# Random-feature attention and a GELU network in one kernel: the instruction order made anew, and sums of weights formed in the x buffer

## The chip, the core and the metric

The kernel runs on one core of a Trainium2 chip. The metric is the time of one execution on the device, in microseconds (us). The engines are PE (TensorE, matrix products), DVE (VectorE), ACT (ScalarE), POOL (GpSimd) and SP (SyncE, which here only issues DMA transfers).

## What is computed

Eight batches of eight heads with 576 tokens of 64 numbers go through attention with exponential features, and the result through a network of two matrix products. Everything is in float32. The core of the reference:

```python
def phi(x):
    proj = np.einsum('bhsd,df->bhsf', x, w_phi)                      # 128 features
    proj = proj - np.max(np.abs(proj), axis=-1, keepdims=True)
    return np.concatenate([np.exp(proj), np.exp(-proj)], axis=-1)
q_p, k_p = phi(q), phi(k)
kv = np.einsum('bhsf,bhsd->bhfd', k_p, v);  z = np.sum(k_p, axis=2)
num = np.einsum('bhsf,bhfd->bhsd', q_p, kv)
den = np.einsum('bhsf,bhf->bhs', q_p, z)[..., None] + 1e-06
x = (num / den) laid out as 4608 tokens of 512
h = x @ w_in;  g = 0.5 * h * (1.0 + erf(h * inv_sqrt2));  out = g @ w_out   # 512 -> 2048 -> 512
```

## The kernel before, in words

**The network** works on 18 blocks of 256 tokens. A number is split into a high part that PE's fast float32 form takes whole and a low rest, so a product is three matrix products (high by high, low by high, high by low). Block j waits for its x: the loads into `xr`, one buffer for all blocks, and of the quotients' denominators into `xh`; then three DVE rows: `xr` times `xh` (L375), a cast to `xh` (L371), and the difference to `xl` (L375). Then, for eight pairs of columns u: `ph_j_u` (24 products of 256 columns), two GELUs on ACT, the difference `gl_j_u` on DVE (it reads `ph`, which is in PSUM), and the second products `po` with `gh`, `gl` and `w_o`. Blocks 8 to 17 (`seven`) form the second product with seven products in place of eight; for that they need five sums or differences of quarters of each pair of `w_o`, 40 in all, which `sums_of_weights` makes earlier, stores in HBM, and `fetch_sums` loads back.

**The weights** `w_in` and `w_out` come as 64-bit numbers in 32 tiles. `split_weight` makes each into two float32r halves: ACT takes the magnitude (L390), DVE does two rows of the form TENSOR_SCALAR (L391, L393) and two of SCALAR_TENSOR_TENSOR (L395, L397) on `wt`, ACT copies the high half (L369), and DVE takes the difference (`w_i..` or `w_o.. <- wt,w`, L375), the last row of a tile.

**The attention** of batch b runs among the blocks: `pk`, `mx`, `ek`, `kv` for the keys, and `pq`, `pc`, `mb`, `ef`, `pn`, `xo` for the queries. `mb` (L511, a maximum over partitions) and, from batch 2 on, `db` (L522, a sum over partitions that gives the denominators) are partition all-reduces on GpSimd. `db` reads `pc` after two TENSOR_SCALAR rows (L553) and two SCALAR_TENSOR_TENSOR rows (L556) of DVE have formed it. A name such as `pc_2_1_0` means batch 2, pair of heads 1, piece 0.

**The order.** The kernel writes down several thousand operations with their reads and writes; `Plan.order` then gives all engines their order by a list schedule with modelled costs and priorities (`rank`), and `emit` issues them so. Each engine runs its own queue strictly in that order on the chip; waits are by semaphores. Of GpSimd and DVE the schedule has a model: `port` is the time at which DVE's last row that works on SBUF alone ends, and `READS` and `SPENT` are how long an all-reduce reads and lasts. A DVE row with `port` that would fall into an all-reduce's reading is put behind it:

```python
if o.eng == "pool" and o.port:
    t = max(t, port[0])
...
if o.eng == "dve" and o.port and port[1] <= t < port[2]:
    t = port[2]
```

Rows of DVE that read PSUM (`mx`, `ek`, `gl`) are made with `port=False`.

Of the kernel before, what the change touches and what calls it, by code (L numbers as in the profile page):

```python
# [62 lines left out]
class Plan:  # L63
# [49 lines left out]
    def order(self, bias):  # L113
# [178 lines left out]
def fused_kernel(ctx: ExitStack, tc: tile.TileContext, qT, kT, va, w_st, w_in, w_out, out):  # L292
# [436 lines left out]
    def sums_of_weights(rank):  # L729
# [3 lines left out]
        for k in range(NFC // 2):  # L733
            d = Buf(plan, None, lambda k=k: dpool.tile([P, 5, 2, HDM], F32, name=f"t_d{k}"))
            stored.append(d)
            a, b = wo[k], wo[k + 8]
            for i, (x, xc, y, yc, o) in enumerate((
                    (b, low_cols, a, high_cols, ALU.add), (b, low_cols, b, high_cols, ALU.add), (a, low_cols, a, high_cols, ALU.add),
                    (b, high_cols, a, high_cols, ALU.subtract), (a, low_cols, b, low_cols, ALU.subtract))):
# [4 lines left out]
                plain, low, high = (lambda t=t: t().bitcast(F32)), (lambda t=t: t()[:, 0, :]), (lambda t=t: t()[:, 1, :])  # L744
# [3 lines left out]
                tt("dve", dve(HDM), low, lambda low=low: low().bitcast(F32), lambda high=high: high().bitcast(F32), ALU.subtract, [t], [t], **kw)  # L748
                op("sp", 0.06, lambda d=d, i=i, plain=plain: nc.sync.dma_start(out=d()[:, i], in_=plain()), r=[t], w=[d], kb=262, **kw)
# [185 lines left out]
```

## Time and profile before

| | us |
|---|---|
| median of 3 runs (lowest, highest) | 1087.42 (1086.15, 1088.69) |
| the profiled execution | 1086.7 |
| its span, first to last instruction | 1084.9 |
| PE busy, share of the span | 1038.2, 96% |
| DVE busy | 697.5, 64% |
| ACT busy | 616.5, 57% |
| POOL busy | 305.4, 28% |

The span is what the trace covers, from the first to the last instruction; the execution's own time is 1.8 us longer. PE is busy nearly all of the time, so the kernel's time is PE's work, plus PE's waits, plus what PE loses while the chip grants it half of its clock.

### The profile page before, as it was taken

Reading aid. Unit: us, or ns where it says so; the run is one execution under the profiler, and the core shown is the slowest. Engines: PE = TensorE matmul, PEld = TensorE weight load, DVE = VectorE, ACT = ScalarE, POOL = GpSimd, SP = SyncE. Lnnn points to the kernel's source line nnn. Section 1 sums busy time; section 2 is a strip of 40 time slices with the busy share of each in tenths; the row PEclk is TensorE's granted clock in tenths of the full one; section 3 lists DMA queues with packets and bytes.
Section 4 is the critical chain, followed back from the end, with each engine's and each line's share of the span. In section 5 each row is a group of like instructions: output and inputs, shape, how many; then the busy total and the mean of one; then the engine's idle time right before and its main releaser. Section 6 shows DMA issues by size and latency. Waiting matters only on the chain.

```text
span 1084.9 us, 23613 instructions
## 1 busy us (share of the span) xinstructions
PE 1038.2 (96%) x9763; PEld 900.0 (83%) x9763; DVE 697.5 (64%) x1228; ACT 616.5 (57%) x1008; POOL 305.4 (28%) x77
## 2 busy tenths in 40 slices
PE   7979995999998999999999999999999999999997
PEld 5646664787786787777788879999999999999997
DVE  5999999688977788665344332555565565565554
ACT  4868785666666687667656653434344344344343
POOL 2232234346556453564654451000000000000000
PEclk7999998999999999999999999999999999999999
DMA  8486660344444335324212145620120120120000
GB/s 285 137 249 190 175 218 27 96 134 134 131 128 130 112 127 146 103 66 124 58 55 75 35 126 173 214 59 20 40 60 11 50 60 16 45 59 20 21 21 21
DMA packets 87180, 107.08 MB, mean 99 GB/s; under 512 B 29168, under 2 KB 56832, under 8 KB 87072
## 3 DMA queue, kind: packets, MB, share of 16 engines
q1 hardware_dynamic: 86928, 105.30, 31.9%
q8 instruction: 77, 1.26, 0.5%
q14 instruction: 31, 0.25, 0.1%
q10 hardware_dynamic: 144, 0.26, 0.1%
HBM read 75.87 MB, written 29.66 MB: 97 GB/s over the span
## 4 chain that ended last, share of the span: by engine, by line
PE 80%; DVE 8%; DMA 4%; ACT 3%; issue 3%; POOL 1%; SPq 0%; DVEq 0%; ACTq 0%; POOLq 0%
PE ph L334 33%; PE po L334 14%; PE pa L334 10%; PE pb L334 7%; PE kv L334 5%; PE pn L334 4%; PE pk L334 2%; PE pq L334 2%; DMA xh<-r_d 1%; DMA x_d<-xo 1%; DVE pc L375 1%; DVE pc L553 1%; DVE ts L375 1%; PE pn_rest L334 1%; POOL mb L511 1%
## 5 line engine op out<-in xcount | busy, mean ns | idle before, releaser
L334 PE MATMUL ph<-xh,w_i 128*128 128x256 f32 x2304 | 419.8, 279 | 7.0 <-DVE w_i L375 5.1
L334 PEld LDWEIGHTS ph<-xh,w_i 128*128 128x128 f32 x2304 | 359.4, 189 | 21.0 <-issue 12.2
L334 PE MATMUL ph<-xl,w_i 128*128 128x256 f32 x1152 | 320.1, 278 | 0.0
L334 PEld LDWEIGHTS ph<-xl,w_i 128*128 128x128 f32 x1152 | 217.9, 189 | 0.3
L522 POOL PARTITION_ALL_REDUCE db<-pc x24 | 151.0, 6290 | 137.2 <-DVE pc L556 112.7
L375 DVE TENSOR_TENSOR sg<-ga 128x256 f32<-128x256 f32 (+1 forms) x240 | 84.6, 376 | 153.2 <-ACT ga L780 151.4
L334 PE MATMUL po<-w_o,gh 128*128 128x512 f32 (+1 forms) x518 | 165.8, 402 | 5.0 <-DVE w_o L375 5.0
L511 POOL PARTITION_ALL_REDUCE mb<-pc x36 | 121.2, 3368 | 161.9 <-ACT pc L369 128.2
L780 ACT ACTIVATE ga<-ph 128x512 f32<-128x512 f32 x80 | 47.8, 598 | 168.7 <-PE ph L334 168.7
L334 PEld LDWEIGHTS po<-w_o,gh 128*128 128x128 f32 x518 | 94.5, 190 | 34.4 <-DVE w_o L375 5.3
L334 PE MATMUL pa<-w_o,oh 128*128 128x256 f32 x640 | 112.8, 276 | 0.0
L334 PE MATMUL po<-w_o,gl 128*128 128x512 f32 (+1 forms) x281 | 102.9, 381 | 7.1 <-DVE gl L375 7.1
L334 PEld LDWEIGHTS pa<-w_o,oh 128*128 128x128 f32 x640 | 96.3, 188 | 0.0
L334 PE MATMUL pa<-w_o,ol 128*128 128x256 f32 x320 | 88.3, 276 | 0.0
L375 DVE TENSOR_TENSOR gl<-ph,gh 128x512 fp32r<-128x512 f32 x64 | 43.7, 685 | 67.5 <-ACT ph L704 67.5
L334 PE MATMUL pn<-ef,kvn 128*64 128x512 f32 (+2 forms) x288 | 80.5, 561 | 5.6 <-ACT xo L369 5.6
L334 PE MATMUL pb<-tw,uh 128*128 128x256 f32 x480 | 85.6, 276 | 0.0
L516 ACT ACTIVATE ef<-pc 128x1024 f32<-128x1024 f32 (+1 forms) x72 | 68.1, 972 | 17.5 <-DVE pc L375 17.2
L444 ACT ACTIVATE ek<-ek 128x1024 f32<-128x1024 f32 x64 | 67.6, 1058 | 15.5 <-DVE ek L375 15.0
L334 PEld LDWEIGHTS pb<-tw,uh 128*128 128x128 f32 x480 | 72.2, 188 | 0.0
L334 PEld LDWEIGHTS po<-w_o,gl 128*128 128x128 f32 x281 | 53.9, 192 | 21.3 <-DVE gl L375 9.6
L703 ACT ACTIVATE gh<-ph 128x512 fp32r<-128x512 f32 x64 | 38.2, 597 | 54.2 <-PE ph L334 52.1
(84 smaller groups left out, 1620.8 us busy)
## 6 DMA issues: line engine op xcount, KB each, us to landing
vt<-in_va_dram SPq DMA_DIRECT2D x32, 325.0 KB
t_d<-ts SPq DMA_DIRECT2D x40, 256.0 KB
out_dram<-ob SPq DMA_DIRECT2D x35, 256.0 KB
kt<-in_kT_dram SPq DMA_DIRECT2D x32, 256.0 KB
raw_i<-in_w_in_dram SPq DMA_DIRECT2D x16, 512.0 KB
raw_o<-in_w_out_dram SPq DMA_DIRECT2D x16, 512.0 KB
qt<-in_qT_dram SPq DMA_DIRECT2D x28, 256.0 KB
x_d<-xo SPq DMA_DIRECT2D x24, 256.0 KB
```

Source lines behind the costliest of these rows:

```text
L334: return tc.keep_in_program_order(nc.tensor.matmul(*a, **kw))
L375: op(eng, cost, lambda: e.tensor_tensor(out=dst(), in0=a(), in1=b(), op=o), r=r, w=w, **kw)
L444: op("act", act(256 * n), lambda s=s: nc.scalar.activation(e[s](), e[1](), AF.Exp, scale=1.0 - 2.0 * s), r=[e[1]], w=[e[s]], table="exp", ...
L511: op("pool", plan.SPENT[most], lambda: nc.gpsimd.partition_all_reduce(mb(), pc(), P, bass_isa.ReduceOp.absmax), r=[pc], w=[mb], port=most, ...
L516: op("act", act(2 * n), lambda s=s: nc.scalar.activation(ef[s](), pc(), AF.Exp, scale=1.0 - 2.0 * s), r=[pc], w=[ef[s]], table="exp", **k())
L522: op("pool", plan.SPENT[total], lambda: nc.gpsimd.partition_all_reduce(db(), pc()[:, :2], P, bass_isa.ReduceOp.add), r=[pc], w=[db], port= ...
L553: op("dve", dve(n, fast=True) + 0.06, lambda pc=pc, ef=ef, one=one, j=j: nc.vector.tensor_scalar(out=pc()[:, j], in0=ef[0]()[:, j], scalar ...
L703: op("act", act(2 * TB, True) + 0.016, lambda gh=gh, ph=ph: nc.scalar.activation(gh(), ph(), AF.Gelu), r=[ph], w=[gh], table="gelu", rank= ...
L780: op("act", act(2 * TB, True) + 0.037, lambda ph=ph, ga=ga: nc.scalar.activation(ga(), ph(), AF.Gelu), r=[ph_all], w=[ga], table="gelu", a ...
```

## The change

Four things change. GpSimd operations no longer wait in the schedule for DVE's port to be free before they start; they start when they are ready, and it is their reading that the schedule moves behind DVE's last row. Their costs are new, and at a tie GpSimd goes first. The sums of weights are formed from whole values: for each pair k two rows `wr_k` add the halves of `w_o k` and `w_o k+8` (512 numbers per partition each) into a buffer of the tag `xr`, the one in which x is scaled; then each of the five sums is one row of 256 from `wr`, the ACT copy, and one difference of 256 (before: one row of 512 straight from the halves and two of 256). Since blocks and sums now share `xr`, the loads of x for block 7 and later wait for the last sum (`behind=last_sum`). And the table of constants is new, so the whole order is. The core of the diff:

```diff
@@ order
-            if o.eng == "pool" and o.port:
-                t = max(t, port[0])
...
-                if best is None or key[1] < best[1]:
+                if best is None or key[1] < best[1] or key[1] == best[1] and e == "pool":
...
-            o.start, o.end = t, run(t, cost, o.duty) if o.eng == "pe" else t + cost
+            o.start = t
+            if o.eng == "pool" and o.port:
+                t = max(t, port[0])
+                port[1:] = [t, t + self.READS[o.port]]
+            o.end = run(t, cost, o.duty) if o.eng == "pe" else t + cost
...
-            clock[o.eng] = o.end + (0.45 if o.eng == "pool" else 0.0)
+            clock[o.eng] = o.end
@@ tokens
-            kw = dict(w=[xr], rank=rank(0) - 8)
+            kw = dict(w=[xr], rank=rank(0) - 8, behind=last_sum if j >= SEVEN - 1 else ())
@@ sums_of_weights, for each k
+            raw = sb["xr"]([P, 4, HDM], F32, f"wr_{k}")
+            plan.since = SUMSAT + SUMSEACH * n
+            for i, w in enumerate((wo[k], wo[k + 8])):
+                tt("dve", dve(2 * HDM), lambda raw=raw, i=i: raw()[:, 2 * i : 2 * i + 2].rearrange("p a t -> p (a t)"),
+                   lambda w=w: w().bitcast(F32)[:, 0], lambda w=w: w().bitcast(F32)[:, 1], ALU.add, [w], [raw], rank=rank(n / 40))
...
-                tt("dve", dve(2 * HDM), plain, lambda x=x, xc=xc: x().bitcast(F32)[:, :, xc], lambda y=y, yc=yc: y().bitcast(F32)[:, :, yc], o, [x, y], [t], **kw)
-                tt("dve", dve(HDM), lambda low=low: low().bitcast(F32), lambda low=low: low().bitcast(F32), lambda high=high: high().bitcast(F32), ALU.add, [t], [t], **kw)
-                copy("act", act(HDM), high, lambda low=low: low().bitcast(F32), [t], [t], **kw)
+                last_sum[:] = [tt("dve", dve(HDM), low, lambda raw=raw, x=x: raw()[:, x], lambda raw=raw, y=y: raw()[:, y], o, [raw], [t], **kw)]
+                copy("act", act(HDM), high, low, [t], [t], **kw)
@@ constants (8 change, two shown)
-SUMSAT = 177.8
+SUMSAT = 224.11
-T0 = 91.27
+T0 = 146.2
```

What the new order is, at three places of DVE's queue. The number at a name's end only counts tiles.

The first place is in block 0, where the last tile of `w_in` (`w_i3_3`) is finished; `ph_0_6` cannot run without it. Before, from the row that completes `pc_2_0_0`, which GpSimd's `db_2_0_0` then reads:

```order
L556 SCALAR_TENSOR_TENSOR pc_2_0_0_1686<-ef_2_0_0_1_1834,kvn_2_0_0_1376,pc_2_0_0_1686 128x512
L395 SCALAR_TENSOR_TENSOR wt_i3_3_1928<-raw_i3_3_1709,wt_i3_3_1928 128x512
L391 TENSOR_SCALAR wt_o12_1946<-wt_o12_1946 128x512
L397 SCALAR_TENSOR_TENSOR wt_i3_3_1928<-raw_i3_3_1709,wt_i3_3_1928 128x512
L393 TENSOR_SCALAR wt_o12_1946<-wt_o12_1946 128x512
L553 TENSOR_SCALAR pc_2_1_0_1729<-ef_2_1_0_0_1843,kvn_2_0_1_1649 128x512
L395 SCALAR_TENSOR_TENSOR wt_o12_1946<-raw_o12_1774,wt_o12_1946 128x512
L375 TENSOR_TENSOR w_i3_3_1959<-wt_i3_3_1928,w_i3_3_1959 128x512
L397 SCALAR_TENSOR_TENSOR wt_o12_1946<-raw_o12_1774,wt_o12_1946 128x512
```

The same place now:

```order
L556 SCALAR_TENSOR_TENSOR pc_2_0_0_1720<-ef_2_0_0_1_1855,kvn_2_0_0_1582,pc_2_0_0_1720 128x512
L375 TENSOR_TENSOR w_i3_3_1937<-wt_i3_3_1838,w_i3_3_1937 128x512
L439 TENSOR_REDUCE mx_2_1_1_1948<-pk_2_1_1_1872 128x8
L375 TENSOR_TENSOR ek_2_1_1_1_1965<-pk_2_1_1_1872,mx_2_1_1_1948 128x1024
L393 TENSOR_SCALAR wt_o12_1885<-wt_o12_1885 128x512
L391 TENSOR_SCALAR wt_o13_1950<-wt_o13_1950 128x512
L395 SCALAR_TENSOR_TENSOR wt_o12_1885<-raw_o12_1715,wt_o12_1885 128x512
L393 TENSOR_SCALAR wt_o13_1950<-wt_o13_1950 128x512
```

`w_i3_3` has moved from the seventh row behind `pc_2_0_0` to the first, and two rows that read PSUM follow it.

The second place is where the last tile of `w_out` (`w_o15`) is finished. Before, `pc_2_1_0`, which `db_2_1_0` reads, had been complete 18 rows ahead of this piece's last row (`db_2_1_0` itself waited for the transfer out of the one `db` buffer):

```order
L397 SCALAR_TENSOR_TENSOR wt_o14_1986<-raw_o14_1870,wt_o14_1986 128x512
L391 TENSOR_SCALAR wt_o15_2084<-wt_o15_2084 128x512
L393 TENSOR_SCALAR wt_o15_2084<-wt_o15_2084 128x512
L395 SCALAR_TENSOR_TENSOR wt_o15_2084<-raw_o15_1949,wt_o15_2084 128x512
L375 TENSOR_TENSOR w_o14_2100<-wt_o14_1986,w_o14_2100 128x512
L397 SCALAR_TENSOR_TENSOR wt_o15_2084<-raw_o15_1949,wt_o15_2084 128x512
L375 TENSOR_TENSOR gl_1_0_2145<-ph_1_0_2070,gh_1_0_2126 128x512
```

The same place now:

```order
L375 TENSOR_TENSOR w_o14_2147<-wt_o14_2091,w_o14_2147 128x512
L397 SCALAR_TENSOR_TENSOR wt_o15_2140<-raw_o15_1931,wt_o15_2140 128x512
L556 SCALAR_TENSOR_TENSOR pc_2_1_0_1752<-ef_2_1_0_1_2094,kvn_2_0_1_1850,pc_2_1_0_1752 128x512
L375 TENSOR_TENSOR xr_2_1511<-xr_2_1511,xh_2_2020 128x1024
L375 TENSOR_TENSOR w_o15_2172<-wt_o15_2140,w_o15_2172 128x512
L556 SCALAR_TENSOR_TENSOR pc_2_1_0_1752<-ef_2_1_0_1_2094,kvn_2_0_1_1850,pc_2_1_0_1752 128x512
L371 CAST xh_2_2020<-xr_2_1511 128x1024
```

The row that completes `pc_2_1_0` now stands behind the last row of `w_o15`. On PE, `kv_2_1_1` and `pn_2_1_0` now stand ahead of the products with `w_o13`, and half of `ph_1_1` (12 products) more ahead of those with `w_o15`.

The third place is where x of block 4 is scaled, in block 3. Before, from the row that completes `pc_4_0_0` (read by `db_4_0_0`):

```order
L556 SCALAR_TENSOR_TENSOR pc_4_0_0_3777<-ef_4_0_0_1_3883,kvn_4_0_0_3399,pc_4_0_0_3777 128x512
L375 TENSOR_TENSOR pc_4_1_0_3832<-pc_4_1_0_3832,mb_4_1_0_3870 128x1024
L375 TENSOR_TENSOR xr_4_3001<-xr_4_3001,xh_4_3745 128x1024
L375 TENSOR_TENSOR gl_3_0_3957<-ph_3_0_3885,gh_3_0_3940 128x512
L439 TENSOR_REDUCE mx_5_0_0_3981<-pk_5_0_0_3959 128x8
```

The same place now:

```order
L375 TENSOR_TENSOR gl_2_7_3766<-ph_2_7_3693,gh_2_7_3740 128x512
L556 SCALAR_TENSOR_TENSOR pc_4_0_0_3576<-ef_4_0_0_1_3720,kvn_4_0_0_3156,pc_4_0_0_3576 128x512
L553 TENSOR_SCALAR pc_4_1_0_3604<-ef_4_1_0_0_3764,kvn_4_0_1_3288 128x512 x2
L556 SCALAR_TENSOR_TENSOR pc_4_1_0_3604<-ef_4_1_0_1_3787,kvn_4_0_1_3288,pc_4_1_0_3604 128x512 x2
L375 TENSOR_TENSOR xr_4_2959<-xr_4_2959,xh_4_3728 128x1024
L375 TENSOR_TENSOR gl_3_0_3856<-ph_3_0_3792,gh_3_0_3844 128x512
```

Between the row that `db_4_0_0` waits for and `gl_3_0` there are now five rows in place of two.

## Rows read from the trace of the kernel before

**Rows 1.** The chain that ended last: share of the span by engine.

```profile
PE 80%; DVE 8%; DMA 4%; ACT 3%; issue 3%; POOL 1%; SPq 0%; DVEq 0%; ACTq 0%; POOLq 0%
```

**Rows 2.** Busy time by stretch: PE, PEld, DVE, ACT, POOL; PE's clock; DMA share, GB/s.

```profile
27.12:162.72 135.60, 122.27 (x1369) 83.06 (x1365) 128.36 (x192) 109.05 (x174) 39.11 (x13) 0.99 0.67 194
162.72:189.84 27.12, 15.07 (x90) 13.51 (x91) 26.37 (x29) 13.81 (x19) 12.41 (x2) 0.80 0.09 28
189.84:325.44 135.60, 134.08 (x1417) 108.57 (x1417) 109.14 (x147) 90.44 (x135) 67.05 (x15) 0.99 0.40 125
325.44:379.68 54.24, 49.86 (x526) 38.98 (x525) 41.83 (x52) 37.16 (x53) 30.06 (x7) 0.94 0.40 121
379.68:678.00 298.32, 296.68 (x2665) 241.38 (x2664) 153.88 (x213) 190.21 (x256) 150.01 (x35) 1.00 0.33 99
678.00:1057.68 379.68, 379.68 (x3353) 379.68 (x3352) 212.51 (x549) 154.36 (x336) 0.00 (x0) 1.00 0.16 50
```

**Rows 3.** PE's timeline: start, us, instruction, and the idle time before it.

```profile
163.33 0.39 PE L334 MATMUL ph<-xh,w_i 128*128 128x256 f32 x1 [1.97 <-ACT w_i L369]
...
168.89 0.79 PE L334 MATMUL ph<-xh,w_i 128*128 128x256 f32 x2 [5.06 <-DVE w_i L375]
...
188.10 0.79 PE L334 MATMUL po<-w_o,gh 128*128 128x512 f32 x1 [5.04 <-DVE w_o L375]
...
195.50 0.74 PE L334 MATMUL po<-w_o,gh 128*128 128x512 f32 x2
...
351.22 0.79 PE L334 MATMUL po<-w_o,gl 128*128 128x512 f32 x1 [4.38 <-DVE gl L375]
```

**Rows 4.** DVE's timeline, in the same form.

```profile
155.65 0.48 DVE L553 TENSOR_SCALAR pc<-ef,kvn 128x512 f32<-128x512 f32 x1
...
162.88 4.76 DVE L553 TENSOR_SCALAR pc<-ef,kvn 128x512 f32<-128x512 f32 x1
...
168.16 0.68 DVE L375 TENSOR_TENSOR w_i<-wt_i,w_i 128x512 fp32r<-128x512 f32 x1
...
180.59 4.56 DVE L391 TENSOR_SCALAR wt_o<-wt_o 128x512 f32<-128x512 f32 x1
185.18 1.54 DVE L393 TENSOR_SCALAR wt_o<-wt_o 128x512 uint32<-128x512 uint32 x1
...
189.39 0.69 DVE L375 TENSOR_TENSOR w_o<-wt_o,w_o 128x512 fp32r<-128x512 f32 x1
...
346.60 3.97 DVE L375 TENSOR_TENSOR xr<-xr,xh 128x1024 f32<-128x1024 f32 x1 [1.51 <-DMA xh<-r_d]
```

**Rows 5.** GpSimd's timeline, in the same form.

```profile
161.17 7.76 POOL L522 PARTITION_ALL_REDUCE db<-pc  x1 [10.73 <-DVE pc L556]
180.24 6.20 POOL L522 PARTITION_ALL_REDUCE db<-pc  x1 [11.31 <-DMA d_d<-db]
```

**Rows 6.** Groups of DVE by shape: count, busy us, mean ns, idle before.

```profile
L375 DVE TENSOR_TENSOR ek<-pk,mx 128x1024 f32<-128x1024 f32 x32 | 39.0, 1219 | 11.3 <-PE kv L334 10.8
L439 DVE TENSOR_REDUCE mx<-pk 128x8 f32<-128x1024 f32 x32 | 39.0, 1218 | 19.7 <-PE pk L334 19.7
...
L375 DVE TENSOR_TENSOR ts<-w_o,w_o 128x512 f32<-128x512 f32 x24 | 19.5, 811 | 1.4 <-DMA t_d<-ts 1.4
```

**Rows 7.** Pieces of the chain that ended last: start, us, products.

```profile
98.19 5.71 PE po L334 x24
...
193.09 2.48 PE kv L334 x80
...
677.58 5.44 PE ph L334 x48
```

**Rows 8.** PE alone, 350 to 356 us: busy time, granted clock, DMA share, GB/s.

```profile
350.00:356.00 6.00, 4.78 (x13) 0.50 0.11 41
```

**Rows 9.** A group of ACT: count, busy us, mean ns, idle before.

```profile
L703 ACT ACTIVATE gh<-ph 128x512 fp32r<-128x512 f32 x64 | 38.2, 597 | 54.2 <-PE ph L334 52.1
```

**Rows 10.** The stores of the sums: issue ns, least, median and most; first and last start.

```profile
L749 SPq DMA_DIRECT2D t_d<-ts x40: 319/326/1021, 201.9 to 443.6; - x40
```

More of the change, by code (lines that the diff above doesn't have):

```diff
@@ L72 @@
     SHAPE = {"f": 0, "k": 1, "q": 1, "v": 2, "n": 2, "w": 3, "d": 4}
-    READS = {"max": 1.12, "add": 2.38, "max main": 1.99, "add main": 4.23, "max rest": 1.0, "add rest": 2.12}
-    SPENT = {"max": 2.28, "add": 3.8, "max main": 3.75, "add main": 6.45, "max rest": 2.07, "add rest": 3.42}
+    READS = {"max": 1.2, "add": 2.45, "max main": 2.15, "add main": 4.45, "max rest": 1.1, "add rest": 2.2}
+    SPENT = {"max": 2.14, "add": 3.59, "max main": 3.54, "add main": 6.11, "max rest": 1.94, "add rest": 3.23}
     WINDOW = 3.413
@@ L223, in order @@
                 left_at[0] = o.end
-            clock[o.eng] = o.end + (0.45 if o.eng == "pool" else 0.0)
+            clock[o.eng] = o.end
             if o.eng == "dve" and o.port:
                 port[0] = o.end
-            if o.eng == "pool" and o.port:
-                port[1:] = [o.start, o.start + self.READS[o.port]]
             for b in o.bufs:
@@ L374, in tt @@
         e = {"dve": nc.vector, "pool": nc.gpsimd}[eng]
-        op(eng, cost, lambda: e.tensor_tensor(out=dst(), in0=a(), in1=b(), op=o), r=r, w=w, **kw)
+        return op(eng, cost, lambda: e.tensor_tensor(out=dst(), in0=a(), in1=b(), op=o), r=r, w=w, **kw)
     def split_weight(src, nm, rank):
@@ L644, in fused_kernel @@
     NU = NFC // 2
+    last_sum = []
     def tokens(j, rank):
@@ L735, in sums_of_weights @@
             stored.append(d)
[L736 to L739, printed above, removed]
+            raw = sb["xr"]([P, 4, HDM], F32, f"wr_{k}")
[3 more added lines that the diff above has]
+                   lambda w=w: w().bitcast(F32)[:, 0], lambda w=w: w().bitcast(F32)[:, 1], ALU.add, [w], [raw], rank=rank(n / 40))
+            for i, (x, y, o) in enumerate(((2, 1, ALU.add), (2, 3, ALU.add), (0, 1, ALU.add), (3, 1, ALU.subtract), (0, 2, ALU.subtract))):
                 kw = dict(rank=rank(n / 40))
@@ L743, in sums_of_weights @@
                 t = sb["ob"]([P, 2, HDM], F32R, f"ts_{k}_{i}")
-                plain, low, high = (lambda t=t: t().bitcast(F32)), (lambda t=t: t()[:, 0, :]), (lambda t=t: t()[:, 1, :])
-                tt("dve", dve(2 * HDM), plain, lambda x=x, xc=xc: x().bitcast(F32)[:, :, xc], lambda y=y, yc=yc: y().bitcast(F32)[:, :, yc], o, [x, y], [t], **kw)
-                tt("dve", dve(HDM), lambda low=low: low().bitcast(F32), lambda low=low: low().bitcast(F32), lambda high=high: high().bitcast(F32), ALU.add, [t], [t], **kw)
-                copy("act", act(HDM), high, lambda low=low: low().bitcast(F32), [t], [t], **kw)
-                tt("dve", dve(HDM), low, lambda low=low: low().bitcast(F32), lambda high=high: high().bitcast(F32), ALU.subtract, [t], [t], **kw)
+                plain, low, high = (lambda t=t: t().bitcast(F32)), (lambda t=t: t()[:, 0, :].bitcast(F32)), (lambda t=t: t()[:, 1, :])
+                last_sum[:] = [tt("dve", dve(HDM), low, lambda raw=raw, x=x: raw()[:, x], lambda raw=raw, y=y: raw()[:, y], o, [raw], [t], **kw)]
+                copy("act", act(HDM), high, low, [t], [t], **kw)
+                tt("dve", dve(HDM), lambda t=t: t()[:, 0, :], low, lambda high=high: high().bitcast(F32), ALU.subtract, [t], [t], **kw)
                 op("sp", 0.06, lambda d=d, i=i, plain=plain: nc.sync.dma_start(out=d()[:, i], in_=plain()), r=[t], w=[d], kb=262, **kw)
@@ L869 @@
 STICK = 2
-PATIENCE = 2.16
+PATIENCE = 3.17
 URGE = -1000.0
-EARLY = 40.11
-WPACE = 4.91
+EARLY = 33.2
+WPACE = 4.89
 WSPAN = 36.41
@@ L878 @@
 ND = 2
-LUMP = 5.52
+LUMP = 6.02
 LINGER = 3.07
@@ L884 @@
 LEAD = 161.66
-HOLD = 13.76
+HOLD = 15.52
 WR = -32.15
@@ L889 @@
 POOLSLACK = 0.3
-DMASLACK = 0.5
-T0 = 91.27
+DMASLACK = 0.26
+T0 = 146.2
 RATE = 285.0
```

## The prediction

> **What bounds the kernel now.** I read the chain that ended last first: four fifths of it is PE, 8% DVE [rows 1]. So the time is PE's work plus PE's waits, and the busy time by stretch says where the waits are [rows 2]. From 678 us to the end PE has not one idle microsecond; the instructions there are the same before and after in kind and number, so that part can only shift. From 190 to 678 us PE lacks 7.5 us: 1.5 and 1.6 us in the two long stretches, 4.4 us between 325 and 380. From 163 to 190 it lacks 12 us of 27, and gets 0.80 of its clock. Before that it lacks 13 us of 136, but there DVE is 95% busy: the weights' tiles come one after the other through DVE, and what PE does in the meantime changes little, because its products end with the last tile.
>
> PE's timeline names the releasers [rows 3]: 1.97 and 5.06 us for tiles of `w_in`, 5.04 us for a tile of `w_out`, and 4.38 us at 351 for a `gl`, all made on DVE. DVE's timeline shows why they were late [rows 4]. At 162.88 a TENSOR_SCALAR took 4.76 us, where the same instruction at 155.65 took 0.48. At 180.59 and 185.18 two such rows took 4.56 and 1.54 us, and at 346.60 the scaling of x took 3.97. Beside the first two GpSimd's timeline has a `db` all-reduce that began at 161.17 and at 180.24 [rows 5]. DVE does not compute for these 4 us; it is held while GpSimd reads. The groups of DVE by shape say which rows are held: the 32 rows `ek` and the 32 rows `mx`, which read PSUM, have the mean of their plain duration, 1.22 us each; the 24 rows `ts<-w_o,w_o`, with both inputs in SBUF, have a mean of 811 ns [rows 6], where `w_i` of the same 512 numbers took 0.68 us [rows 4]. So a hold costs DVE some 4.3 us (4.76 - 0.48) unless rows that read PSUM stand there, and it costs PE what the held row's followers were needed for.
>
> The Trainium skill (SBUF — State Buffer, Who interferes with whom) has the same pair in conflict, but lets the one that comes first keep the port for its whole instruction. Here DVE came free after 4.6 us of an all-reduce of 6.2 us, so the measurement decides; by the page's rule the hold that stays near `w_i3_3` (below) would be about 1.9 us longer and the sum 1071.
>
> **The change, part by part.**
>
> *The last weight tiles.* Before, `w_o15`'s last row began at 189.39 us on DVE [rows 4]. The new queue has the same rows ahead of it but for three: the last `pc_2_1_0` row and `gl_1_0` (0.7 us each) come after it, and the scaling of x of block 2 (1.2 us) comes ahead. That is nothing net. What differs is the holds. The second (4.56 + 1.54 - 2 x 0.48 = 5.1 us) goes: `db_2_1_0` reads `pc_2_1_0`, and the row that completes it now stands behind `w_o15`. The first (4.28 us) stays, since `db_2_0_0` is still released ahead; but the rows that now follow are `w_i3_3`, which is issued in the same breath as the row that releases GpSimd, and then `mx` and `ek`, 2.44 us that are not held [rows 6]. What is left of the hold is 1.8 us. So the row begins at 189.39 - 4.28 - 5.1 + 1.84 = 181.8 and ends 0.7 later; PE started 0.05 us after such an end at 168.89. PE reaches the products with `w_o15` at 182.6, if it is not late itself.
>
> Is it? From the end of `w_i3_3` it has to do 75 first products (5.44 us for 48, so 8.5 us), 12 second products (5.71 for 24: 2.9), `kv` (2.48), `pn` (not more) and a small `pk`: 17 us at the most [rows 7]. `w_i3_3` began at 168.16 behind a hold; without the hold 163.9, and several rows fewer stand ahead of it. 163.9 + 0.7 + 17 = 181.6. It is not late. Before, PE was at these products at 195.50 [rows 3]. That is 12.9 us earlier, and 12 of block 1's products (half of `ph_1_1`, 1.36 us) are done that were not: **14.3 us**.
>
> *Block 3.* At 351 PE waited 4.38 us, and then ran at half clock: granted 0.50 from 350 to 356, which is the 1.2 GHz level, while it was busy 4.78 of 6 us [rows 8]. Half of that is lost too, 2.4 us. The cause was `db_4_0_0`: it held the scaling of x, and `gl_3_0` stood right behind. Now the row that releases `db_4_0_0` stands behind `gl_2_7`, and the hold falls on rows of `pc_4_1_0`. From there to `gl_3_0` DVE has some 7.5 us (a hold of 4.3, two rows of 0.4, two of 0.7, the 1.2 of x); PE has four `po` pieces of 6, two of attention and `ph_3_0` between, some 11 us. `gl_3_0` is then not late: **6.8 us**.
>
> *The sums of weights.* 24 rows of 512 numbers fewer on DVE, 0.7 us each, some 16 us of work. Behind 189 us PE does not wait for DVE's amount of work (64 to 80% busy there), so this is worth nothing by itself. The cover is PE's queue of products; if a stretch lost that cover, a row would cost its 0.7 us. That the sums start later (behind x of block 4, not of block 2) thins DVE's queue between 190 and 325 us, where it was 80% busy, and fills it from there to about 580, where it was 52 to 77%.
>
> *The shared buffer.* Sums 0 to 14 stand between the scalings of x of blocks 4 and 5, sums 15 to 39 between blocks 6 and 7, and x of block 7 loads only after the last sum. Its three rows are the last on DVE before `ph_7_0`: counted from the end of `ph_6_7`, two GELUs of 0.6 us [rows 9], `gl_6_7` of 0.7 and the hand-overs are about 2.4 us, x times r, cast, one more row and the difference 1.2 + 0.7 + 1.2 + 1.2 less what rows overlap, about 4.1; together 6.5 us, against two `po` pairs and a `pn` on PE, 7.5 us. One microsecond of slack, and the loads also stand in SP's queue behind the transfer out of `db_7_1_0`.
>
> *New waits.* No row shows what the new order makes PE wait. Nothing is the one bound; a wait as at 351 with its slow clock, 6.8 us, the other. The small waits that PE has between 190 and 325 and behind 380 sum to 3.1 us [rows 2]; I take 3.0 more, nearest to these, for block 7's start and for holds of about 20 more `db`.
>
> *Sum.* 14.3 + 6.8 - 3.0 = 18.1 us less. On the profiled execution, 1086.7 us (its span 1084.9 and 1.8 around it), that is 1068.6; the median of the runs shown is 0.7 above, so **1069.3 us**.
>
> **The rivals.**
>
> *A hold lands on a row that PE waits for.* `w_i3_3`'s last row needs ACT's copy. If that is not there when `pc_2_0_0` is complete, GpSimd goes first, `w_i3_3` waits the 4.3 us, and `mx` and `ek` no longer cover the hold: 2.4 us for `w_o15`, and up to 2.4 more for a slow clock. For it: ACT is 80% busy from 27 to 163 us [rows 2]. Against: the copy's input is ready two rows (1.2 us) ahead, and before, `w_i3_3` had no idle time of DVE ahead of it [rows 4]. One hold in blocks 3 to 6 that PE feels as at 351 is 6.8 us. That gives 1072 to 1081, about 1075.
>
> *The sums become the bound (slower).* Before, the 40 sums went out in 242 us, 6.0 us each [rows 10]. Now 25 of them stand between blocks 6 and 7, where PE has 12 `ph`, 26 `po` of 6 and about 28 us of attention: 97 us, 3.9 us per sum. Each sum holds one of two `ob` buffers over an ACT copy and a store, and ten `db` hold DVE there. At 5.0 us each x of block 7 is 125 - 98 = 27 us late and the kernel takes 1096; it is slower than before from 4.7 us on. Against: DVE waited 1.4 us in all for a store of sums [rows 6]; the old pace is that at which the table of constants releases them (`SUMSEACH`, 5.81), not that of the transfers.
>
> *The order gives nothing.* Each wait that goes comes back elsewhere: 1087. The 12 us between 163 and 190 have a cause that is gone in the queue, so this is unlikely.
>
> **How the numbers follow.** Forecast 0.62 (1062 to 1072), a hold on the path 0.24 (1072 to 1081), nothing gained 0.05, the sums as bound 0.09. The low end is the forecast without new waits and with the small ones gone (1063), less a little for `mb` holds that may be hidden as well; the high end is both holds of the first rival, 1081, and a little. Range 1060 to 1083. A change of 0.2% (2.2 us) is about what a measurement of this kernel can tell from none: faster 0.87, same 0.04, slower 0.09.
>
> **What would show it.** PE at the products with `w_o15` near 183 us and no wait of 4 us or more between 160 and 200; granted clock 1.00 there; DVE rows of 4 us and more on `pc` and `ts` still, but none on a `wt_o` row behind 175; no PE wait above 1.5 us in the first quarter of block 3; x of block 7 scaled just before `ph_7_0`. It is wrong if PE idles before `ph_0_6` as long as before, if `w_o15` ends after 187, or if PE stands for several microseconds before `ph_7_0`.

## The result and the profile after

| | before | after |
|---|---|---|
| median of 4 runs, us | 1087.76 | 1073.85 |
| lowest to highest | 1086.15 to 1088.69 | 1072.37 to 1075.91 |
| ratio, 95% interval | | 0.9875 (0.9855 to 0.9895) |
| span of the profiled execution | 1084.9 | 1070.6 |

The kernel is 13.9 us faster; 18.1 were forecast, and the time lies within the range. First the busy time by stretch, which answers to [rows 2]: after the stretch, PE, PEld, DVE, ACT and POOL, then the granted clock, the DMA share and GB/s.

```profile
162.72:189.84 27.12, 24.61 (x213) 20.13 (x211) 22.51 (x33) 20.59 (x30) 9.87 (x3) 0.94 0.26 77
189.84:325.44 135.60, 132.08 (x1461) 106.38 (x1462) 81.96 (x88) 88.26 (x117) 76.19 (x18) 1.00 0.30 86
325.44:379.68 54.24, 53.79 (x535) 42.47 (x532) 42.16 (x55) 41.36 (x60) 30.49 (x6) 1.00 0.39 122
379.68:678.00 298.32, 294.29 (x2600) 242.47 (x2599) 186.35 (x261) 176.33 (x259) 140.29 (x33) 0.99 0.41 130
```

From 163 to 190 us PE lacks 2.5 us where it lacked 12.1; from 325 to 380 it lacks 0.45 where it lacked 4.4. In the two other stretches it lost more than before: 3.5 us where it was 1.5, 4.0 where it was 1.6. PE's timeline says where. These are the long waits behind 160 us. Among them is the start of the products with `w_o15` (183.04), the row that answers to 195.50 in [rows 3].

```profile
167.61 0.58 PE L334 MATMUL ph<-xh,w_i 128*128 128x256 f32 x1 [2.51 <-DVE gl L375]
...
183.04 0.62 PE L334 MATMUL po<-w_o,gh 128*128 128x512 f32 x2
...
242.28 0.72 PE L334 MATMUL pk_r<-wst,kr 64*128 64x128 f32 x8 [1.77 <-DVE ek L375]
...
262.57 1.13 PE L334 MATMUL pq<-qt,wst 64*128 64x512 f32 x4 [1.13 <-issue]
...
511.82 0.80 PE L334 MATMUL po<-w_o,gl 128*128 128x512 f32 x1 [2.80 <-DVE gl L375]
```

None of the four waits of [rows 3] is left. Two new ones of more than 2 us end with a `gl` row, and behind each of them PE had half of its clock, 0.51 and 0.50, which is the 1.2 GHz level. Two stretches of the trace show it, with the columns as above:

```profile
167.00:170.50 3.50, 2.89 (x13) 2.89 (x14) 3.50 (x6) 2.60 (x3) 0.00 (x0) 0.51 0.41 124
512.00:515.20 3.20, 3.20 (x8) 2.52 (x9) 1.56 (x3) 3.14 (x4) 0.47 (x1) 0.50 0.22 83
```

DVE's timeline shows what stood ahead of the two `gl` rows (166.88 and 511.09), and when `w_o15` was ready (180.06, the row that was at 189.39 in [rows 4]):

```profile
162.15 2.30 DVE L393 TENSOR_SCALAR wt_o<-wt_o 128x512 uint32<-128x512 uint32 x1
164.37 1.65 DVE L391 TENSOR_SCALAR wt_o<-wt_o 128x512 f32<-128x512 f32 x1
...
166.88 0.68 DVE L375 TENSOR_TENSOR gl<-ph,gh 128x512 fp32r<-128x512 f32 x1
...
180.06 0.69 DVE L375 TENSOR_TENSOR w_o<-wt_o,w_o 128x512 fp32r<-128x512 f32 x1
...
507.75 3.41 DVE L375 TENSOR_TENSOR ts<-wr 128x256 f32<-128x256 f32 x1 [1.56 <-DMA t_d<-ts]
511.09 0.68 DVE L375 TENSOR_TENSOR gl<-ph,gh 128x512 fp32r<-128x512 f32 x1
```

GpSimd's timeline has an all-reduce `db` beside each, as [rows 5] had:

```profile
159.26 6.48 POOL L522 PARTITION_ALL_REDUCE db<-pc  x1 [4.96 <-DVE pc L556]
...
506.35 6.11 POOL L522 PARTITION_ALL_REDUCE db<-pc  x1 [4.55 <-DVE pc L556]
```

At 167 the held rows are only a part of the wait. `gl_0_6` also reads what ACT makes of `ph_0_6`, and ACT, which had to do an `ek` and load a table of functions first, had that ready at 165.73; the `gl` row began 1.15 us later. ACT's timeline:

```profile
163.35 1.28 ACT L704 ACT_TABLE_LOAD   x1
164.64 0.60 ACT L704 ACTIVATE gh<-ph 128x512 fp32r<-128x512 f32 x1
165.14 0.59 ACT L705 ACTIVATE ph<-ph 128x512 f32<-128x512 f32 x1
```

The second case is the one to read closely. `ts_3_2`'s first row stood at the head of DVE's queue and waited 1.56 us for the store of an earlier sum, since the sums share two buffers. In that time GpSimd, which had been released at 506.2, began to read. The row takes 0.42 us when nothing is in its way (the median below); here it took 3.41, and `gl_5_3`, whose input had been there since 504.7, stood behind it. The group of these rows in the second bunch of sums, then their stores, which answer to [rows 10] (count; ns least, median, most; first and last start):

```profile
L375 DVE TENSOR_TENSOR ts<-wr x25: 411/417/3416, 497.1 to 591.9; 128x256 f32<-128x256 f32 x25
...
L751 SPq DMA_DIRECT2D t_d<-ts x25: 319/320/552, 503.6 to 594.1; - x25
```

The 25 stores went out in 90.5 us, 3.8 us apart. x of block 7 came in time: its last row ended at 606.34, and `ph_7_0` began at 607.60 without a wait.

```profile
605.12 1.22 DVE L375 TENSOR_TENSOR xl<-xr,xh 128x1024 fp32r<-128x1024 f32 x1
```

### The profile page after: what moved, and what is told of

Its sections match the earlier page's. It is cut to its first block, busy times and chain, and to the rows that moved or that the text cites. A ratio compares the mean times of both kernels' runs of the same rounds, so it can differ in the third digit from the quotient of the medians.

```text
span 1070.6 us, 23592 instructions
## 1 busy us (share of the span) xinstructions
PE 1034.1 (97%) x9760; PEld 895.5 (84%) x9760; DVE 689.0 (64%) x1204; ACT 605.1 (57%) x998; POOL 305.1 (28%) x77
## 4 chain that ended last, share of the span: by engine, by line
PE 79%; DVE 10%; DMA 4%; issue 3%; ACT 2%; SPq 1%; DVEq 0%; ACTq 0%
PE ph L334 33%; PE po L334 14%; PE pa L334 10%; PE pb L334 7%; PE kv L334 5%; PE pn L334 4%; PE pk L334 2%; PE pq L334 2%; DVE mx L439 1%; DMA t_d<-ts 1%; DMA dc<-d_d 1%; DVE pc L375 1%; DVE ek L375 1%; DMA x_d<-xo 1%; DVE wt_i L395 1%
## 5 line engine op out<-in xcount | busy, mean ns | idle before, releaser
L334 PE MATMUL ph<-xh,w_i 128*128 128x256 f32 x2304 | 415.5, 278 | 2.8 <-DVE gl L375 2.5
L334 PEld LDWEIGHTS ph<-xh,w_i 128*128 128x128 f32 x2304 | 356.7, 188 | 14.1 <-issue 8.3
L444 ACT ACTIVATE ek<-ek 128x1024 f32<-128x1024 f32 x64 | 67.7, 1058 | 17.1 <-DVE ek L375 16.4
L334 PE MATMUL kv<-vt,ek 128*64 128x65 f32 x2048 | 65.5, 222 | 1.4 <-ACT ek L444 1.4
```

What stands on the lines that cost most here:

```text
L334: return tc.keep_in_program_order(nc.tensor.matmul(*a, **kw))
L444: op("act", act(256 * n), lambda s=s: nc.scalar.activation(e[s](), e[1](), AF.Exp, scale=1.0 - 2.0 * s), r=[e[1]], w=[e[s]], table="exp", ...
```

## The experiments

The theory is that of the prediction: what the order changed is which rows stand on DVE while GpSimd reads, and a held row costs what stands behind it. Its rivals: DVE's smaller amount of work is the gain; the waits have another cause; the table of numbers alone makes the gain. Unless the text says otherwise, a ratio is to the kernel before in the same series, whose median was 1086.7, 1087.4 and 1087.9 us in the three series; the kernel after was timed in a series of its own, above.

### Which rows are held, and for how long

`e1` is a kernel of its own, the loop below; `kinds` holds the eight kinds of row, and `src`, which GpSimd reads, is written by the row ahead.

```python
for op in (bass_isa.ReduceOp.add, bass_isa.ReduceOp.absmax):
    for k, f in kinds.items():
        keep(v.tensor_tensor(out=src, in0=red, in1=b, op=ALU.subtract))
        keep(g.partition_all_reduce(red, src, P, op))
        for i in range(rows[k]):
            keep(f())
```

> This kernel leaves out the whole computation and measures the hold by itself: beside a running all-reduce of 128x1024 numbers on GpSimd (sum, then largest magnitude) DVE does rows of one kind after another, 8 kinds, with the dependence that only the first row of each kind waits for GpSimd. Theory of the hold: the kinds whose operands all lie in SBUF (two inputs 128x512, the TENSOR_SCALAR rows, three operands, the cast) have one long row of about 4.3 us more than its plain duration beside the sum and about 2 us more beside the largest magnitude; the kinds that read PSUM (difference of 512, of 1024, the reduction) have none, at most 0.1 us more. Rival, the rule that whoever has the port keeps it for the whole instruction: the long row is as long as the all-reduce, 6.1 us and 3.5 us. Rival, contention for memory: every row beside GpSimd is some 10 to 50% longer and none is long by itself, PSUM or not.

Measured, one line of the answers by source line for each kind (count; ns least, median, most; first and last start): seven of the kinds beside the sum, then two beside the largest magnitude; the lines left out repeat the pattern. `a`, `b`, `u` and `w` lie in SBUF, `x` in PSUM.

```profile
L66 DVE TENSOR_TENSOR c<-a,b x14: 684/692/4907, 10.7 to 24.4; 128x512 f32<-128x512 f32 x14
L70 DVE TENSOR_SCALAR c<-a x24: 422/427/4639, 26.1 to 42.1; 128x512 f32<-128x512 f32 x24
L72 DVE SCALAR_TENSOR_TENSOR u<-w,u x14: 684/693/4907, 60.9 to 74.6; 128x512 uint32<-128x512 uint32 x14
L73 DVE CAST r<-a x24: 420/427/4642, 76.3 to 92.3; 128x512 fp32r<-128x512 f32 x24
L66 DVE TENSOR_TENSOR c<-x,a x14: 684/691/692, 93.8 to 103.2; 128x512 f32<-128x512 f32 x14
L75 DVE TENSOR_TENSOR c<-x,m x8: 1218/1224/1224, 104.9 to 113.7; 128x1024 f32<-128x1024 f32 x8
L77 DVE TENSOR_REDUCE m<-x x8: 1218/1224/1224, 116.0 to 124.8; 128x8 f32<-128x1024 f32 x8
...
L66 DVE TENSOR_TENSOR c<-a,b x14: 683/692/2553, 127.1 to 138.4; 128x512 f32<-128x512 f32 x14
L70 DVE TENSOR_SCALAR c<-a x24: 418/427/2289, 140.1 to 153.6; 128x512 f32<-128x512 f32 x24
```

Read the most against the median: 4907 - 692 = 4215 ns, 4639 - 427 = 4212 ns beside the sum; 1861 and 1862 ns beside the largest magnitude. The kind does not matter as long as it is one that is held, and the three kinds that read PSUM have no long row at all (their most is at most 1 ns above the median). The all-reduces took 6.1 to 6.5 and 3.5 to 3.9 us, so the rival of the whole instruction falls. With it falls, in this one point, the rule of the Trainium skill that was weighed in the prediction (SBUF — State Buffer, Who interferes with whom). Its other points agree: a row with one operand in SBUF and one in PSUM is not held, the casts and TENSOR_SCALAR rows are. The rival of contention falls too: it asked for rows that are all somewhat longer, and for none that is long by itself.

### Both kernels without the long reads

`e2` is the kernel before, `e3` the kernel after, both with this edit; `db` is one buffer, filled with ones at the start, so that the transfers behind it read something.

```diff
-            mb(), pc(), P, bass_isa.ReduceOp.absmax), r=[pc], w=[mb], port=most, **k(1))
+            mb()[:, :, :16], pc()[:, :, :16], P, bass_isa.ReduceOp.absmax), r=[pc], w=[mb], port=most, **k(1))
-        tt("dve", dve(2 * n), pc, pc, mb, ALU.subtract, [pc, mb], [pc], **k(1))
+        tt("dve", dve(2 * n), pc, pc, lambda: mb()[:, :, :1].to_broadcast([P, 2, n]), ALU.subtract, [pc, mb], [pc], **k(1))
-        ... nc.gpsimd.partition_all_reduce(db(), pc()[:, :2], P, ...
+        ... nc.gpsimd.partition_all_reduce(db()[:, :, :16], pc()[:, :2, :16], P, ...
```

> The kernel before, in the same order on PE, DVE and ACT, with all-reduces that read and write 16 columns in place of 288 to 512 for each head; so the largest magnitude and the sum over partitions are left out for the other columns. Theory of the hold: the four long waits (1.97, 5.06 and 5.04 us between 163 and 188, 4.38 at 351) and their slow clock go, 16 to 20 us: 1067 to 1072 us, and it stands within 6 us of the kernel after treated in the same way. Rival, that the 24 DVE rows fewer are the gain: it stands 10 us or more above the kernel after treated so, since the rows are still there. Rival, that the waits have another cause (the weights' loads, ACT): 1083 to 1088 with the waits at 163 to 190 in place.

> The kernel after, treated as the one before: all-reduces of 16 columns, the same order on PE, DVE and ACT. Theory of the hold: what is left of holds goes, the wait of 2.51 us at 167.6 in part and the one of 2.80 at 511.8 with its slow clock, 5 to 9 us: 1065 to 1069 us. Rival, that the order after has no cost of holds left and waits for other things: 1072 to 1075 us, with the wait at 511 in place.

Measured: `e2` 1061.85 us, ratio 0.9771 (0.9756 to 0.9786); `e3` 1057.47 us, 0.9724 (0.9708 to 0.974). The stretches of `e2`, then of `e3` from 163 to 325 us, columns as above:

```profile
162.72:189.84 27.12, 25.46 (x236) 23.12 (x236) 21.14 (x34) 20.65 (x29) 1.09 (x2) 0.94 0.24 69
189.84:325.44 135.60, 135.60 (x1451) 108.80 (x1450) 93.48 (x155) 94.15 (x142) 10.14 (x17) 1.00 0.43 132
325.44:379.68 54.24, 53.35 (x554) 41.86 (x553) 38.47 (x60) 42.01 (x58) 3.92 (x6) 1.00 0.39 122
```

```profile
162.72:189.84 27.12, 26.28 (x228) 20.19 (x225) 20.45 (x31) 21.62 (x31) 1.72 (x3) 1.00 0.32 97
189.84:325.44 135.60, 135.60 (x1483) 110.07 (x1482) 68.64 (x95) 91.91 (x123) 10.56 (x17) 1.00 0.33 91
```

With the order of before untouched, PE's 12.1 us of idle time from 163 to 190 shrink to 1.7: the waits of 5.06 and 5.04 us were the hold's (0.79 and nothing are left of them). The 1.97 ahead of them, for ACT's copy of `w_i`, was not, since 1.71 of it stay just ahead of the stretch. Nor was all of the wait at 351. In `e2`, too, the scaling of x waits for the transfer of the denominators, and `gl_3_0` behind it; 0.89 us are left. DVE's and PE's timelines:

```profile
330.57 1.23 DVE L375 TENSOR_TENSOR xr<-xr,xh 128x1024 f32<-128x1024 f32 x1 [1.50 <-DMA xh<-r_d]
```

```profile
332.45 0.50 PE L334 MATMUL po<-w_o,gl 128*128 128x512 f32 x1 [0.89 <-DVE gl L375]
```

The kernel before loses 24.9 us with the reads, the kernel after 16.4 (1073.85 - 1057.47, from two series), and without them the two stand 4.4 us apart. So most of the 13.9 us, some 8.5, goes with the reads and is what the new order avoids; the rival of DVE's work, which asked for 10 us or more between the two, falls. What the 4.4 us come from was not tried. Both gains are larger than expected: the small waits between 190 and 678 went as well, down to none from 190 to 325. The edit also shortens each all-reduce itself, to 0.5 to 1.5 us, so a part may be that results come sooner; the two were not told apart.

### One row moved in the order of before

Three kernels are the kernel before with its order taken as planned, and then one row of DVE moved; PE, ACT and GpSimd keep theirs.

```diff
-        todo = sorted(self.done, key=lambda o: (o.start, o.n))
+        todo = rearranged(sorted(self.done, key=lambda o: (o.start, o.n)))
```

In `e4`, `gl_3_0` goes ahead of the scaling of x for block 4; in `e5`, that scaling goes behind `gl_3_0`, `mx_5_0_0` and `ek_5_0_0`; in `e6`, the last row of `pc_2_1_0` goes behind the last row of `w_o15`.

> The kernel before with one row of DVE moved by one place: gl_3_0 ahead of the scaling of x for block 4. Theory of the hold: gl_3_0 reads PSUM, so it is not held, and the 4.38 us that PE waited at 351 and the half clock behind it go: 6.8 us less, 1080 to 1082 us; the scaling of x stays held for 4 us, and nobody waits for it. Rival, that a wait that goes comes back elsewhere: within 2 us of the kernel before.

> The kernel before with one row of DVE moved by three places: the scaling of x for block 4 behind gl_3_0, mx_5_0_0 and ek_5_0_0, which read PSUM. In the run with gl_3_0 alone ahead, mx and ek still stood behind the held row, and PE waited 2.00 us for what ACT makes of ek and 0.86 and 1.14 us later. Theory of the hold: the three rows fill the time in which GpSimd holds the rest, so that PE waits for none of them: 6 to 7 us less than before, 1080 to 1081 us. Rival, that the waits at 358 and 363 come from ACT's queue and not from ek: like the run with gl_3_0 alone, 1083 us.

> The kernel before with one row of DVE moved, the last one of pc_2_1_0 behind the last row of w_o15 (its all-reduce db_2_1_0 and the transfers that follow go later with it; PE, ACT and GpSimd keep their order). Theory of the hold: the rows of w_o14 and w_o15 are no longer held at 180.6 and 185.2, and the wait of 5.04 us at 188 with its slow clock goes: 6 to 7 us less, 1080 to 1081 us; the hold falls on the scaling of x for block 2, for which nobody waits. The waits at 163 and 169 stay. Rival, that PE would then wait at 188 for something else, or that x of block 2 comes late: 1085 to 1088 us.

Measured: `e4` 1083.32 us, 0.9963 (0.9951 to 0.9975); `e5` 1081.16, 0.9944 (0.9929 to 0.9959); `e6` 1080.26, 0.9937 (0.9923 to 0.9952). `e4` gave half of what was expected: the wait at 351 went, and 2.00 us came back at 358 because `mx` and `ek` stood behind the held row. DVE's and PE's timelines of `e4`:

```profile
346.09 4.07 DVE L375 TENSOR_TENSOR xr<-xr,xh 128x1024 f32<-128x1024 f32 x1 [0.81 <-DMA xh<-r_d]
350.08 1.21 DVE L439 TENSOR_REDUCE mx<-pk 128x8 f32<-128x1024 f32 x1
351.32 1.22 DVE L375 TENSOR_TENSOR ek<-pk,mx 128x1024 f32<-128x1024 f32 x1
```

```profile
358.46 1.97 PE L334 MATMUL kv<-vt,ek 128*64 128x65 f32 x60 [2.00 <-ACT ek L444]
```

In `e5` they go first, and the same scaling takes 1.95 us in place of 4.07, because the rows that read PSUM have filled the hold:

```profile
347.81 1.23 DVE L439 TENSOR_REDUCE mx<-pk 128x8 f32<-128x1024 f32 x1 [0.53 <-PE pk L334]
349.07 1.23 DVE L375 TENSOR_TENSOR ek<-pk,mx 128x1024 f32<-128x1024 f32 x1
350.21 1.95 DVE L375 TENSOR_TENSOR xr<-xr,xh 128x1024 f32<-128x1024 f32 x1
```

That is 6.2 us for one row in another place, which is the prediction's 6.8 for block 3 measured by itself. It is the price of all that stood ahead of `gl_3_0`: the hold (3.97 - 1.22 = 2.75 us) and the transfer that the scaling had waited for (1.51 us, in the last row of [rows 4]). The rival of `e5`, ACT's queue, falls: the wait of 2.00 us is gone with `ek` moved. `e6` is 7.1 us, the second hold ahead of `w_o15` by itself. In its trace the hold falls on the cast of x for block 2, and PE has no wait of 0.3 us or more between 170 and 260:

```profile
188.14 4.43 DVE L371 CAST xh<-xr 128x1024 fp32r<-128x1024 f32 x1
```

The rivals of `e4` and `e6`, that a wait comes back elsewhere, fall, for `e4` by half.

### The parts of the change apart

`e7` takes the table of numbers alone, `e10` the planner's rules for GpSimd alone, `e12` the new sums alone, and `e8` all but the sums. Their diffs are the hunks of the change; of each one line:

```diff
# e7 and e8
-T0 = 91.27
+T0 = 146.2
# e10 and e8
-            if o.eng == "pool" and o.port:
-                t = max(t, port[0])
# e12
-            a, b = wo[k], wo[k + 8]
+            raw = sb["xr"]([P, 4, HDM], F32, f"wr_{k}")
```

> The kernel before with the new table of numbers alone (SUMSAT, PATIENCE, EARLY, WPACE, LUMP, HOLD, DMASLACK, T0); the planner's rules for GpSimd and the sums of weights are those of before. In its order db_2_1_0 is released three rows ahead of w_o15's last row and db_2_0_0 ahead of four rows of w_o13 to w_o15. Theory of the hold: both holds still delay the last weight tiles, so a wait of 3 us or more stands between 160 and 200: 1077 to 1086 us. Rival, that the table is what makes the kernel faster: 1072 to 1076 us.

> The kernel after with the sums of weights as they were (five rows from the weight tiles with a row of 512 numbers each, no use of x's buffer, x of block 7 not held back); the planner's rules and the table are the new ones, so DVE has the 24 rows of 512 numbers more. Its order is that of after up to block 2. Theory of the hold: 1070 to 1078 us, within 4 us of the kernel after, with no wait of 4 us between 160 and 200. Rival, that DVE's smaller amount of work is the gain: 1084 us or more.

> The kernel before with the planner's new rules for GpSimd alone (an all-reduce may start when its input is ready, goes first on equal times, new times of reading and of the whole); the table and the sums are those of before. In its order the row that releases db_2_1_0 stands ahead of all rows of w_o12 to w_o15 but two. Theory of the hold: a wait of 3 us or more between 160 and 200 stays, since the order around the last weight tiles needs both; 1080 to 1092 us. Rival, that the rules alone make the gain: 1076 us or less.

> The kernel before with the new sums of weights alone (in x's buffer), rules and table of before. In its order 35 of the 40 sums stand between the scalings of x for blocks 6 and 7. The stores of the second bunch of sums in the kernel after followed each other at 3.8 us (25 of them from 503.6 to 594.1). Theory: 35 sums take 133 us where PE has some 97 us of work, so x of block 7 is some 36 us late and PE stands there: 1105 to 1135 us, slower than before. The waits between 160 and 190 stay, since the order is the same up to there. Rival, that the 24 rows of DVE fewer make the kernel faster: 1075 to 1086 us.

| rules | table | sums | us | ratio (95%) |
|---|---|---|---|---|
| new | old | old | 1079.47 | 0.9924 (0.9904 to 0.9943) |
| old | new | old | 1101.35 | 1.0126 (1.0107 to 1.0145) |
| new | new | old | 1068.67 | 0.9831 (0.9811 to 0.985) |
| old | old | new | 1120.04 | 1.0288 (1.0257 to 1.0318) |
| new | new | new | 1073.85 | 0.9875 (0.9855 to 0.9895) |

The new sums with only one of the other two parts were not run. The table alone makes the kernel slower, by more than expected: a wait of 6.05 us stands at 181, for a `gl` that DVE made behind a held weight tile (4.76 us for a TENSOR_SCALAR row at 172.29). But the expectation priced only the stretch up to 200. Waits of 2.75 and 4.44 us for `gl` rows follow at 415 and 492, and the attention ends so late that block 8 waits:

```profile
692.36 0.80 PE L334 MATMUL pa<-w_o,oh 128*128 128x256 f32 x2 [6.45 <-ACT oh L369]
```

The rules alone give 8.4 us, with a wait of 3.51 us at 184 left, as expected; the time is half a microsecond below the range. With them PE still lacks 7.1 us from 163 to 190, at 0.75 of its clock; with rules and table (`e8`) it lacks 2.7, at 1.00. `e8` is the surprise: 1070 to 1078 us were expected, and it lies 1.3 us below. With the old sums, and 24 rows of 512 numbers more on DVE, the kernel is about 5 us faster than the kernel after, and the two intervals do not overlap; the rival of DVE's amount of work falls. From 380 to 678 its PE is busy 296.94 us, 2.6 more than in the kernel after:

```profile
379.68:678.00 298.32, 296.94 (x2714) 246.62 (x2713) 162.45 (x246) 188.99 (x264) 145.00 (x34) 1.00 0.38 119
```

`e12` shows the rival in which the sums become the bound, at about the price expected: 32 us slower, where 36 us of lateness were worked out. 35 sums stand between blocks 6 and 7 there, x of block 7 is late, and PE waits for attention and then for x. PE's timeline:

```profile
638.47 3.68 PE L334 MATMUL pn<-ef,kvn 128*64 128x512 f32 x8 [11.34 <-ACT ef L516]
...
659.37 0.58 PE L334 MATMUL ph<-xh,w_i 128*128 128x256 f32 x1 [9.67 <-DVE xh L371]
```

### Rows moved in the order of after

`e9` is the kernel after with `gl_5_3` ahead of the row of `ts_3_2` that waited for a store. `e11` is `e8` with four rows moved in the same manner.

> The kernel after with one row of DVE moved by one place: gl_5_3 ahead of the first row of ts_3_2. In the profile after, that row waited 1.56 us for the store of an earlier sum, GpSimd's sum db_6_1_0 came first and held the row for 3 us, and PE waited 2.80 us for gl_5_3 behind it and then had half clock for 3.4 us. Theory, that a sum's row which waits for a store in DVE's queue is what the shared stretch costs: 4 to 5 us less than the kernel after, 1069 to 1070 us, most of the distance to the kernel without the new sums. Rival, that the wait comes back behind (the sums later, x of block 7 late): 1072 us or more.

> The kernel after with the old sums of weights (1068.7 us), and four rows of DVE moved: two TENSOR_SCALAR rows of w_o12 and w_o13 behind gl_0_6, and the scaling of x for block 4 with one row of a sum behind gl_3_1. Theory: a gl row reads PSUM and is not held, so it must not stand behind a row that is held or that waits for a transfer; the wait of 2.65 us at 167 becomes shorter by 1.1, the one of 2.03 at 325 and its slow clock go: 4 to 5 us less, 1063 to 1066 us. Rival, that a wait that goes comes back elsewhere: 1067 us or more.

Measured: `e9` 1071.09 us, 0.985 (0.9823 to 0.9877); `e11` 1064.93 us, 0.9791 (0.9775 to 0.9807). In `e9`'s trace the wait of 2.80 us and the slow clock behind it are gone, and the same row of `ts_3_2` takes 4.45 us, now behind the `gl`:

```profile
504.06 0.68 DVE L375 TENSOR_TENSOR gl<-ph,gh 128x512 fp32r<-128x512 f32 x1
504.67 4.45 DVE L375 TENSOR_TENSOR ts<-wr 128x256 f32<-128x256 f32 x1
```

The time is 2.8 us less than that of the kernel after, where 4 to 5 were expected, and the intervals overlap, so the size is not settled. As in `e4`, an `ek` stood behind the held row, and waits of 0.54, 0.47 and 0.75 us for it came back between 510 and 514; and ahead of the edit, where the order is the same, a `pq` waited 2.57 us at 259.52 that had waited 1.13 at 262.57. `e11` is the fastest kernel that computes the whole, at the expected time and 8.9 us below the kernel after. Its trace gives the moves less than was worked out. Of the 2.65 us that `e8` waited at 167, 1.55 stay: nothing on DVE holds `gl_0_6` any more, which stands 3.53 us at the head of the queue for ACT. DVE's and PE's timelines:

```profile
165.42 0.69 DVE L375 TENSOR_TENSOR gl<-ph,gh 128x512 fp32r<-128x512 f32 x1 [3.53 <-ACT ph L704]
```

```profile
166.17 0.39 PE L334 MATMUL ph<-xh,w_i 128*128 128x256 f32 x1 [1.55 <-DVE gl L375]
```

And 1.07 us came back at 172, for a `w_o` tile; the 2.03 at 325 and the slow clock are gone, and 1.59 came back at 334. The profiled spans are 1064.8 and 1063.0, nearer to each other than the medians: `e8`'s four runs lie between 1066.64 and 1071.3, and the profiled one is the fastest. So the trace shows for 325 us alone that a move helps, and its size is uncertain.

## Why the prediction was right, and where its sum was off

**What bounds the kernel**: right in the main. Most of the waits came from DVE rows that are held while GpSimd reads, for 4.2 us beside the sum in `e1` (4.3 was read from one row), and rows that read PSUM are exempt. Two readings gave the hold too much. The 1.97 us at 163 ended with ACT's copy, as its row in [rows 3] says, and not with a row of DVE. And of the 4.38 at 351 the hold alone is 2.75; the scaling of x had first waited 1.51 us for a transfer, and without the long reads 0.89 us stay (`e2`). Neither changes the sum, since the new order took both causes away. Beside the second sum DVE did not come free after 4.6 us: one row passed, and the next was held for 1.1 more [rows 4]. And DVE was 52 to 80% busy in the stretches behind 189 us, not 64 to 80%.

**The last weight tiles**, 14.3 us: right. PE is at the products with `w_o15` at 183.04 (forecast 182.6), 12.5 us earlier, with the 12 products of `ph_1_1` (1.36 us) done ahead of them: 13.8. But the last to come was PE, not DVE. `w_o15` was ready at 180.75, 1.7 us sooner than worked out; among the reasons is that the row that releases `db_2_0_0` began at 158.43, where it had begun at 160.34 before, and `w_i3_3` behind it at 159.09, where 163.9 was worked out. PE was 2.3 us behind `w_o15` because of its wait at 167.61 and the half clock up to 170.5. So two errors nearly cancel, and that the forecast is met within half a microsecond is luck; that both holds' waits went is not. The hold behind `mx` and `ek` kept 3.1 us (2.30 + 1.65 - 2 x 0.41), where 1.84 were worked out, and fell on two rows ahead of `gl_0_6`.

**Block 3**, 6.8 us: right. 3.9 us of idle time and 2.4 of slow clock are gone; `e5` measured 6.2 by itself.

**New waits**, 3.0 us: mis-sized, and this is the step that failed. In the two long stretches between 190 and 678 PE idles 7.5 us where it idled 3.1, and 1.6 us went to half clock behind 511: 6.0 us. The sum then is 13.8 + 6.3 - 6.0 = 14.1 of the 14.3 by which the spans differ. I had taken the value nearest to the waits that were there, so one hold that PE feels was priced in the rival and not in the sum. That rival (a hold on a row that PE waits for) is what happened at 511, where it cost 4.4 us with the half clock, and in part at 167: 1.1 us of that wait are the held rows' (2.65 in `e8`, 1.55 in `e11`), the rest is ACT's.

**The sums**, worth nothing by themselves: wrong in sign. In this order they cost about 5 us (`e8`). The cover that the prediction named, PE's queue of products, is there for the amount of work; what it does not cover is a row at the head of DVE's queue that waits for a store, during which GpSimd gets in first. Shown for one place, 511 us, by the timelines and in part by `e9`; whether the rest of the 5 us has the same cause stays open, since the orders of `e8` and of the kernel after differ from block 2 on. Of the 5.8 us between their profiled spans some 1.4 are not the sums' at all: they are the half clock behind 167, where the order is the same and `e8` had its full clock.

**The shared buffer**: right. `ph_7_0` had 1.3 us of slack (one was forecast), and the sums went at 3.8 us where, by the prediction, 4.7 would have made the kernel slower. `e12` shows what lies beyond.

**What would show it**: the forecast of PE's clock, 1.00 from 160 to 200, was wrong for 3.5 us, and no row of `ts` took 4 us or more (the longest 3.56), while rows of `pc` did (4.16 at 253.81). The others came out, the largest wait from 160 to 200 being 2.51.

## What to carry to other kernels

A wait on an engine is felt by what stands behind it in the queue: before moving or saving work, see which rows stand behind one that can be held or that waits for a transfer, and put those that PE needs ahead of it. Rows that read PSUM are the ones to set beside a GpSimd all-reduce; one row in another place was worth 6 to 7 us here, and 24 rows less of DVE's work gave no gain that showed. And where a planner's rules and its table of numbers are made together, one without the other says little: the table alone cost 14 us.

## What the runs showed of the hardware

In `e1` the hold has a length that depends on GpSimd's operation and not on the held row: 4.21 us beside the sum of 128x1024 numbers, 1.86 beside the largest magnitude, to within 4 ns over rows of 0.43 and 0.69 us. One row took all of it there. In the kernels two rows can share it, so a row can pass in the middle, and together they can lose more: 3.1 us at 162 in the kernel after, behind rows that read PSUM, but 5.3 (4.56 + 1.54 - 2 x 0.42) at 180.59 in the kernel before [rows 4]. Why was not tried.

A wait does not always bring the slow clock: after 2.51 us at 167 the kernel after had 0.51 of its clock, while `e8`, with the same order there and 2.65 us of waiting, had 1.00 in the whole stretch (PE's timeline, then the busy time):

```profile
166.85 0.39 PE L334 MATMUL ph<-xh,w_i 128*128 128x256 f32 x1 [2.65 <-DVE gl L375]
```

```profile
162.72:189.84 27.12, 24.46 (x214) 19.00 (x213) 22.72 (x33) 20.63 (x30) 11.19 (x3) 1.00 0.28 81
```

So the same wait can differ by what half clock costs, here some 1.4 us (2.89 us busy at 0.51).
